# S4 tables and a sliding-window attention on one core: factors on GpSimd, absolute values by a mask, exponentials and sines in a fixed order, projections dealt over all table steps

## The chip, the cores and the metric

The kernel runs on one core of one Trainium2 chip. The core has five engines with queues of their own: PE (TensorE, matrix products into PSUM), DVE (VectorE), ACT (ScalarE, functions by activation tables), POOL (GpSimd) and SP (SyncE, which issues transfers), and 16 DMA engines. The metric is the device time of one execution in microseconds (us), the median of several runs.

## The reference

Two independent parts are computed and laid side by side in the output (2048 x 1152).

Part A is attention over a window: `qkv = x @ wqkv` with 2048 rows, 576 columns and 32 heads of 18, then for each row a softmax over itself and the 255 rows before it, and `o @ wo`.

Part B is a convolution by a state-space model, 576 channels with 128 states each:

```
dt = exp(log_dt);  logdA = dt * (A_re + i A_im);  dB = dt * (B_re + i B_im)
P[d, n, l] = exp(logdA[d, n] * l)                    l = 0 .. 2047
K[d, l]    = real( sum over n of C[d, n] * P[d, n, l] * dB[d, n] )
y          = causal convolution of u with K, per channel (by FFT), + u * Dskip
```

The exponent is complex, so each element of P needs an exponential (real part) and a sine and a cosine (imaginary part).

## The kernel before, in words

**Two stages.** The first stage computes, at the same time, the projections q, k, v (`proj`), the kernel K of the convolution (`tables`) and the first step of the transform of u (`s1_u`). When K is complete, `s1_k` transforms it and writes it to HBM (`gk`). The second stage runs attention and the rest of the convolution, in an order written out by hand.

**Tables.** The time index is split as l = 64 a + m, so that P is a product of two small tables. The 576 channels are worked in 18 groups of 32, here called pairs, each of two chunks of 16 channels (36 chunks, numbered c). For a pair there are factors A and tr (12 values of a per channel, with the weights C dB multiplied in); for a chunk there is Q (64 values of m, real and imaginary). The steps of one chunk:

- `outer` (L314): PE multiplies log-rates by index values and gives the exponents in PSUM, in one of two buffers (x).
- `exps_ab` (L334) and `exps_q` (L344): ACT takes exponentials of the real parts, for two pairs and four chunks at a time, into mab (3 buffers) and mg (4).
- `fraction` (L324 to L326): ACT rounds the phase to an integer k, DVE subtracts it (f), and ACT takes the absolute value ab with Abs. The sine of f and the cosine, as sine of pi/2 - |2 pi f|, follow on ACT (L356 and L357 for a pair, L395 and L396 for a chunk).
- `factors` (L358 to L369): six DVE operations make tr (768 elements per partition), t1 and t2 (256 each) and the three parts of A (128 each).
- `products` (L380): POOL multiplies A by tr into two tiles m of 1024 elements (pool P, two buffers of each).
- `qtable` (L400 to L403): DVE multiplies sines and cosines, which lie in PSUM, by mg into Q (two buffers).
- `taps` (L418): PE sums over the 128 states, 128 small matmuls a chunk as the trace counts them, into kp, one PSUM buffer for both chunks of a pair; ACT then copies kp into K (L424).

**Projections.** x comes in four column blocks. For each block ACT and DVE make a scaled half-precision pair xh and xl (L226 to L229); the scale needs the largest value of all of x, which goes over the partitions with an all-reduce on POOL (L144). Then there are nine steps for q and k (14 matmuls of width 512 each, L172, evicted by ACT at L236 and DVE at L237, six stores of about 0.6 us of issue on SP) and four for v (28 matmuls of width 288, evicted by ACT at L248, one store). They share three PSUM buffers (pps) with `s1_u` (L461). With the block's loading that makes 14 steps a block, 56 in all.

**What sets the order.** Every function is a Python generator that yields after a step, and `merge` picks the next step from the generator that has gone through the smallest share of the steps named for it:

```
merge((part(proj, 16), 16), (part(tables, 20), 20), (part(s1u, 4), 4))
merge((proj, 56), (tables, 400), (s1u, 12))
```

This gives a program order. A scheduler, which runs when the kernel is built, then fixes each engine's own queue from it: an instruction goes in as its inputs and its buffer become free by the scheduler's clock, earlier ones in the program first. On the chip every engine runs its queue strictly in that order. An activation table is loaded (ACT_TABLE_LOAD, 1.283 us) where an exponential follows a sine in ACT's queue, or a sine an exponential.

The number 400 in the second merge is the steps that `tables` is taken to have; it has 304 after the first 20.

Of the kernel before, what the change touches and what calls it, by code (L numbers as in the profile page):

```python
# [13 lines left out]
I32 = mybir.dt.int32  # L14
AF = mybir.ActivationFunctionType
OP = mybir.AluOpType
# [14 lines left out]
TWO_PI = 6.283185  # L31
# [71 lines left out]
class Kernel:  # L103
# [214 lines left out]
    def fraction(self, x, pool, n, w):  # L318

        nc = self.nc  # L320
        k = pool.tile([128, n * w], I32, name="k")
        f = k.bitcast(F32)
        ab = pool.tile([128, n * w], F32, name="ab")
        nc.scalar.activation(k, x, AF.Copy)  # L324
        nc.vector.tensor_tensor(f, x, k, op=OP.subtract)  # L325
        nc.scalar.activation(ab, f, AF.Abs)  # L326
        return f, ab

    def exps_ab(self, s):

        for q in (2 * s, 2 * s + 1):
            x = self.outer(self.al, q, [self.mul["c_ca"]], 0, GC)
            m = self.p["mab"].tile([128, GC, 12], F32, name="mab")
            self.nc.scalar.activation(m, x.rearrange("p (c m) -> p c m", m=12), AF.Exp)  # L334
            self.mab[q] = m
            yield

    def exps_q(self, s):

        for c in range(4 * s, 4 * s + 4):  # L340
            mg = self.p["mg"].tile([128, HC, 64], F32, name="mg")
            for e in range(2):
                x = self.outer(self.al, c // 2, [self.mul["c_cm"]], c % 2 * HC + e * 8, 8)
                self.nc.scalar.activation(mg[:, e * 8:e * 8 + 8], x.rearrange("p (c m) -> p c m", m=64), AF.Exp)  # L344
                yield
            self.mg[c] = mg

    def factors(self, q):

        nc, tt, pool = self.nc, self.nc.vector.tensor_tensor, self.p["ab"]  # L350
        x = self.outer(self.ps, q, [self.mul["c_ca"], self.mul["c_cp"]], 0, GC)
        f, ab = self.fraction(x, self.p["abt"], GC, 12)
        yield
        tr = pool.tile([128, GC, 2, 12], F32, name="tr")
        v = lambda z: z.rearrange("p (c m) -> p c m", m=12)
        nc.scalar.activation(tr[:, :, 1, :], v(f), AF.Sin, scale=TWO_PI)  # L356
        nc.scalar.activation(tr[:, :, 0, :], v(ab), AF.Sin, scale=-TWO_PI, bias=self.halfpi)  # L357
        tt(tr, tr, self.mab.pop(q).unsqueeze(2).to_broadcast([128, GC, 2, 12]), op=OP.mult)  # L358
        yield
        t1 = self.p["abt"].tile([128, GC, 2, 4], F32, name="t1")  # L360
        t2 = self.p["abt"].tile([128, GC, 2, 4], F32, name="t2")
        sh = [128, GC, 2, 4]
        w = lambda z: z[:, q * GC:q * GC + GC].unsqueeze(2).unsqueeze(3).to_broadcast(sh)
        tt(t1, tr[:, :, :, 8:12], w(self.wr), op=OP.mult)
        tt(t2, tr[:, :, :, 8:12], w(self.wi), op=OP.mult)
        A = pool.tile([128, GC, 12], F32, name="A")
        tt(A[:, :, 4:8], t1[:, :, 0], t2[:, :, 1], op=OP.subtract)
        tt(A[:, :, 8:12], t2[:, :, 0], t1[:, :, 1], op=OP.add)
        nc.vector.scalar_tensor_tensor(A[:, :, 0:4], t2[:, :, 0], -1.0, t1[:, :, 1], op0=OP.mult, op1=OP.subtract)  # L369
        self.AB[q] = A, tr  # L370
        yield

# [16 lines left out]
    def qtable(self, c):  # L389
        nc, tt = self.nc, self.nc.vector.tensor_tensor  # L390
        f, ab = self.fr.pop(c)
        sn = self.p["trig"].tile([128, HC, 32], F32, name="sn")
        cs = self.p["trig"].tile([128, HC, 32], F32, name="cs")
        v = lambda z: z.rearrange("p (c m) -> p c m", m=32)
        nc.scalar.activation(sn, v(f), AF.Sin, scale=-TWO_PI)  # L395
        nc.scalar.activation(cs, v(ab), AF.Sin, scale=-TWO_PI, bias=self.halfpi)  # L396
        yield
        m = self.mg.pop(c)
        Q = self.p["Q"].tile([128, HC, 2, 64], F32, name="Q")
        tt(Q[:, :, 0, 32:64], cs, m[:, :, 32:64], op=OP.mult)  # L400
        tt(Q[:, :, 0, 0:32], cs[:, :, ::-1], m[:, :, 0:32], op=OP.mult)  # L401
        tt(Q[:, :, 1, 32:64], sn, m[:, :, 32:64], op=OP.mult)
        nc.vector.scalar_tensor_tensor(Q[:, :, 1, 0:32], sn[:, :, ::-1], -1.0, m[:, :, 0:32],  # L403
                                       op0=OP.mult, op1=OP.mult)
        self.Q[c] = Q
# [20 lines left out]
    def tables(self):  # L426
        self.mab, self.mg, self.AB, self.P, self.fr, self.Q = {}, {}, {}, {}, {}, {}
        yield from self.exps_ab(0)
        yield from self.exps_ab(1)
        yield from self.exps_q(0)  # L430
        yield from self.factors(0)
        self.products(0)
        self.phases(0)
        yield
        n = 2 * NQ
        for c in range(n):
            if c % 2 == 0 and c // 2 + 1 < NQ:
                yield from self.factors(c // 2 + 1)
            if c + 1 < n:
                self.products(c + 1)  # L440
                self.phases(c + 1)
                yield
            yield from self.qtable(c)
            yield
            if c % 4 == 3 and c + 1 < n:
                if c + 5 < n:
                    yield from self.exps_ab(c // 4 + 2)
                yield from self.exps_q(c // 4 + 1)
            if c:
                yield from self.taps(c - 1)  # L450
        yield from self.taps(n - 1)


# [489 lines left out]
    def build(self):  # L943
        nc, a = self.nc, self.a
        with ExitStack() as es:
            self.pool(es, "const", 1)
            self.pool(es, "dram", 1, DRAM)
            self.pool(es, "dram2", 2, DRAM)
            cp, dp = self.p["const"], self.p["dram"]
            self.w1 = cp.tile([128, 2, 128], F32, name="w1")  # L950
            nc.gpsimd.dma_start(self.w1, a["c_w1"])
            self.gx = dp.tile([2, 64, 128, 144], F32, name="gx")
            self.gk = dp.tile([2, 64, 128, 144], F32, name="gk")
            self.h = dp.tile([2, 64, 32, D], F32, name="h")
            with ExitStack() as ek:
                self.pool(ek, "K", 1)
                with ExitStack() as e1:
                    for n, b, s in (("s4c", 1, None), ("pps", 3, PSUM), ("xps", 2, PSUM), ("trig", 1, PSUM),
                                    ("kps", 1, PSUM)):
                        self.pool(e1, n, b, s)  # L960
                    with ExitStack() as e2:
                        self.pool(e2, "prep", 1)
                        self.s4_prep()
                    for n, b in (("wq", 1), ("raw", 2), ("x", 1), ("pst", 2), ("s1u", 2), ("s1s", 2), ("ab", 2), ("abt", 1), ("mab", 3),
                                 ("mg", 4), ("fr", 2), ("Q", 2), ("P", 2)):
                        self.pool(e1, n, b)
                    proj, tables, s1u = self.proj(), self.tables(), self.s1_u()
                    merge((part(proj, 16), 16), (part(tables, 20), 20), (part(s1u, 4), 4))
                    merge((proj, 56), (tables, 400), (s1u, 12))
                with ExitStack() as e1:  # L970
                    self.pool(e1, "s1s", 2)
                    self.pool(e1, "s1p", 3, PSUM)
                    for _ in self.s1_k():
                        pass
            with ExitStack() as e1:
                self.pool(e1, "fc", 1)
                self.i2 = self.p["fc"].tile([128, 64], F32, name="i2")
                nc.sync.dma_start(self.i2, a["c_i2"])
                self.dsk = self.p["fc"].tile([128, D], F32, name="dsk")
                nc.sync.dma_start(self.dsk, a["dsk"].partition_broadcast(128))  # L980
                for n, b, s in (("fs", 2, None), ("fy", 2, None), ("att", 1, None), ("m", 2, None), ("P", 4, None),
                                ("v", 4, None), ("o", 3, None), ("n", 2, None), ("n1", 1, None), ("h7", 1, None), ("wo", 1, None), ("wo2", 2, None),
                                ("stp", 2, PSUM), ("ops", 1, PSUM), ("ring", 3, PSUM)):
                    self.pool(e1, n, b, s)
                self.att_setup()
                with self.tc.manual_schedule():
                    self.attention(self.conv())
# [35 lines left out]
```

## Time and profile before

| | |
|---|---|
| median of 3 runs | 1079.5 us (1076.2 to 1081.78) |
| the profiled execution | 1075.61 us, of which the span on the core is 1073.6 |
| PE busy | 857.8 us (80% of the span) |
| DVE busy | 736.2 us (69%) |
| ACT busy | 619.9 us (58%) |
| POOL busy | 511.1 us (48%) |
| mean granted clock of PE | 0.946 |
| ACT table loads from 30 to 475 us | 35, of 1.283 us each |

A busy share is an average over both stages and says little of either. PE's matmuls overlap in the pipeline and their ends are modelled, so a busy PE is not a PE at its peak; its real work is counted better from runs of back-to-back matmuls. The chain of waits follows the work that ended last backwards: at each step to what released it, or to the instruction before it on its engine. A row of one source line gives the shortest, median and longest duration in ns, the times of the first and last start, and the shape. A line of waits reads: who waited, for whom, us in total, how often, the longest.

### The profile page before, as it was taken

How to read it: one execution, taken by the hardware profiler on the slowest of the kernel's cores; microseconds unless marked ns; L12 is line 12 of the kernel's file. 1: busy time of each engine (PE TensorE's matmuls, PEld its weight loads, DVE VectorE, ACT ScalarE, POOL GpSimd, SP SyncE). 2: the span in 40 equal slices, each digit the busy share in tenths (PEclk: the TensorE clock that was granted, in tenths of full speed). 3: DMA queues.
4: the chain of work that ended last, by engine and by line, in shares of the span. 5: the costliest groups of instructions: out<-in, count | busy, mean ns of one | idle time of the engine just before them, and what ended most of it. 6: DMA issues, size and time to landing. Idle time of an engine off the chain costs nothing.

```text
span 1073.6 us, 26801 instructions
## 1 busy us (share of the span) xinstructions
PE 857.8 (80%) x10332; PEld 450.7 (42%) x10332; DVE 736.2 (69%) x1859; ACT 619.9 (58%) x955; POOL 511.1 (48%) x606
## 2 busy tenths in 40 slices
PE   1535879897988797987578888878888899988787
PEld 0313436554744464553234333333333344434345
DVE  2879685669576845226676788888878766767564
ACT  1776758776797784233146655566566656644471
POOL 0004344435452632010235677766876666666770
PEclk9966989998998998999889999999999999999999
DMA  9665423442344232588616456454645644579763
GB/s 271 168 184 160 105 53 88 109 94 59 85 111 96 55 74 64 130 217 239 188 49 180 138 147 175 147 148 127 176 113 177 185 118 142 146 185 256 204 190 121
DMA packets 155911, 152.27 MB, mean 142 GB/s; under 512 B 36856, under 2 KB 134392, under 8 KB 155592
## 3 DMA queue, kind: packets, MB, share of 16 engines
q1 hardware_dynamic: 148152, 131.98, 45.3%
q0 software_dynamic: 6128, 14.60, 5.4%
q10 hardware_dynamic: 1504, 3.99, 1.3%
q8 instruction: 81, 1.33, 0.6%
q14 instruction: 46, 0.38, 0.1%
HBM read 89.12 MB, written 61.01 MB: 140 GB/s over the span
## 4 chain that ended last, share of the span: by engine, by line
PE 37%; DVE 25%; ACT 10%; DMA 10%; issue 9%; POOL 5%; SPq 2%; DVEq 0%; ACTq 0%; POOLq 0%
PE pp L172 8%; PE r L636 4%; PE po L700 4%; PE r L903 4%; PE r L500 4%; PE kp L418 4%; PE pp L461 3%; DVE jk L643 3%; POOL P L688 2%; DMA gk<-g 2%; PE ST L677 2%; PE x L314 2%; PE r L508 2%; DVE tr L358 2%; ACT P L679 2%
## 5 line engine op out<-in xcount | busy, mean ns | idle before, releaser
L643 DVE CUSTOM_DVE_ANT_0 jk<-r,bias 128x288 f32<-128x288 f32 (+7 forms) x512 | 198.0, 433 | 88.7 <-PE r L636 88.0
L679 ACT ACTIVATE P<-ST,esc 128x1024 f32<-128x1024 f32 (+1 forms) x192 | 202.0, 1059 | 92.9 <-PE ST L677 92.1
L380 POOL TENSOR_TENSOR m<-A,tr 128x1024 f32<-128x1024 f32 x72 | 149.5, 2098 | 194.2 <-PE kp L418 139.1
L688 POOL TENSOR_SCALAR_AFFINE_SELECT P<-P 128x512 f32<-128x512 f32 x240 | 171.7, 745 | 103.2 <-ACT P L679 100.8
L636 PE MATMUL r<-K,qb 128*64 128x288 f16 (+7 forms) x1024 | 130.5, 297 | 36.7 <-DVE qb L627 10.7
L700 PE MATMUL po<-P,V 128*32 128x256 f32 (+2 forms) x1408 | 100.2, 395 | 17.5 <-POOL P L688 8.1
L418 PE MATMUL kp<-Q,m 128*32 128x64 f32 x4608 | 88.3, 230 | 27.6 <-DVE Q L401 10.0
L636 PEld LDWEIGHTS <-qb 128*64 128x64 f16 x1024 | 60.3, 109 | 119.3 <-issue 65.6
L536 POOL TENSOR_TENSOR Y<-t,t 64x288 f32<-64x288 f32 x64 | 53.5, 835 | 109.8 <-DVE t L531 107.8
L418 PEld LDWEIGHTS kp<-Q,m 128*32 128x32 f32 x4608 | 75.2, 116 | 56.3 <-issue 41.7
L461 PE MATMUL pp<-ut,w 128*128 128x288 f32 x128 | 52.8, 538 | 40.9 <-DMA ut<-in_u_dram 18.6
L677 PE MATMUL ST<-Q,K 64*128 64x384 f16 (+2 forms) x704 | 73.5, 280 | 3.0 <-DMA Q<-mt 2.9
L237 DVE SCALAR_TENSOR_TENSOR qst<-pp,qst 128x512 f16<-128x512 f32 x36 | 24.7, 685 | 64.7 <-ACT qst L236 61.8
L128 ACT ACTIVATE g<-pp 128x288 f32<-128x288 f32 (+1 forms) x84 | 34.5, 447 | 40.4 <-DMA gk<-g 22.0
L700 PEld LDWEIGHTS po<-P,V 128*32 128x32 f32 x1408 | 35.7, 110 | 52.5 <-issue 25.7
L537 POOL TENSOR_TENSOR Y<-t,t 64x288 f32<-64x288 f32 x64 | 54.5, 852 | 3.8
L461 PEld LDWEIGHTS pp<-ut,w 128*128 128x128 f32 x128 | 28.9, 245 | 61.1 <-issue 24.1
L326 ACT ACTIVATE ab<-k 128x512 f32<-128x512 f32 (+1 forms) x54 | 31.9, 590 | 37.0 <-DVE k L325 36.6
L172 PE MATMUL pp<-xh,wh 128*128 128x512 f16 x180 | 47.9, 388 | 1.2 <-DVE xh L229 1.2
L172 PEld LDWEIGHTS <-wh 128*128 128x128 f16 x324 | 32.0, 101 | 39.3 <-issue 6.6
L172 PE MATMUL pp<-xh,wl 128*128 128x512 f16 x180 | 48.3, 392 | 0.0
L500 PE MATMUL r<-tx,w 128*64 128x288 f32 x256 | 40.2, 430 | 9.9 <-DMA tx<-gx 8.7
(177 smaller groups left out, 1756.1 us busy)
## 6 DMA issues: line engine op xcount, KB each, us to landing
gx<-g SPq DMA_DIRECT2D x32, 288.0 KB
qd<-qst SPq DMA_DIRECT2D x72, 128.0 KB
gk<-g SPq DMA_DIRECT2D x16, 576.0 KB
tx<-gx SPq DMA_DIRECT2D x16, 576.0 KB
tk<-gk SPq DMA_DIRECT2D x16, 576.0 KB
h<-ho SPq DMA_DIRECT2D x16, 576.0 KB
raw<-in_xT_dram SPq DMA_DIRECT2D x16, 512.0 KB
Q<-qd SPq DMA_DIRECT2D x32, 216.0 KB
```

The lines of the kernel that those rows point to most:

```text
L172: self.nc.tensor.matmul(ps, u, v, start=(i == 0), stop=(i == len(ops) - 1))
L380: self.nc.gpsimd.tensor_tensor(m, A[:, ch, a0:a0 + 8].unsqueeze(3).to_broadcast(sh), tr[:, ch, part, 0:8].unsqueeze(2).to_broadcast(sh), o ...
L418: nc.tensor.matmul(kp[32 * st:32 * st + 32, c % 2 * JJ2 + j, :], m[:, ch, a0:a0 + 32], Q[:, ch, term % 2, :], start=(term == 0), stop=(ter ...
L461: nc.tensor.matmul(ps, self.w1[:, part, :], src[:, o:o + k], start=True, stop=True)
L500: nc.tensor.matmul(ps[64 * par:64 * par + 64], w2[:, par, 64 * part:64 * part + 64], t[:, 2 * hs:2 * hs + 2, par, :], start=True, stop=True)
L537: nc.gpsimd.tensor_tensor(Y[par][64:128], t1[sl, 1], t2[sl, 1], op=OP.add)
L636: nc.tensor.matmul(ps[64 * b:64 * b + 64, :n], self.qb[:, b, t, :], d["K"][:, b, k0:k0 + n], start=True, stop=True, skip_group_check=True)
L643: nc.vector.tensor_tensor_reduce(out=jk[:, :n], in0=ps[:, :n], in1=self.bias[:, 288 - n:], scale=1.0, scalar=-3e38, op0=OP.add, op1=OP.max ...
L677: nc.tensor.matmul(ps[:, u, o:o + n], d["K"][h, jp, k0:k0 + 128], d["Q"][h, jp, q0:q0 + n], start=True, stop=True, skip_group_check=True)
L679: nc.scalar.activation(pt[:, 2 * jp:2 * jp + 2, lo:hi], ps[:, :, lo:hi], AF.Exp, scale=self.esc)
L688: nc.gpsimd.affine_select(v, v, pattern=[[0, 4], [sg, 128]], compare_op=OP.is_ge, fill=0.0, base=-1 if far else 0, channel_multiplier=-sg)
L700: nc.tensor.matmul(self.po[32 * j:32 * j + 32, t0 * 128:t1 * 128], V[:, kb * 76 + 19 * j:kb * 76 + 19 * j + 32], pt[:, j, o:o + (t1 - t0) ...
```

## The change

It has five parts. In `fraction` the absolute value is no longer taken by ACT (Abs) but by DVE, as a bitwise mask that clears the sign. All exponentials and sines of the tables go through a helper `act`, which gives them a token that keeps them in program order on ACT. In `factors` the five two-input operations run on POOL in place of DVE, and the sixth, a scaled subtraction of two tiles, becomes the negative of the part just made (one input). `products(c + 1)` stands behind `taps(c - 1)` in the program, no longer ahead of `phases(c + 1)`. The pool mab has four buffers, and the merge is told 304 steps of tables instead of 400.

```diff
 def fraction(self, x, pool, n, w):
...
-        nc.scalar.activation(ab, f, AF.Abs)
+        nc.vector.tensor_scalar(ab.bitcast(I32), k, 0x7FFFFFFF, None, op0=OP.bitwise_and)
...
+    def act(self, *args, **kw):
+
+        self.tc.stamp_issue_order_token(self.nc.scalar.activation(*args, **kw).ins, "transcendentals")
...
 def exps_ab(self, s):
-            self.nc.scalar.activation(m, x.rearrange("p (c m) -> p c m", m=12), AF.Exp)
+            self.act(m, x.rearrange("p (c m) -> p c m", m=12), AF.Exp)
...
 def factors(self, q):
-        nc, tt, pool = self.nc, self.nc.vector.tensor_tensor, self.p["ab"]
+        nc, tt, pool = self.nc, self.nc.gpsimd.tensor_tensor, self.p["ab"]
...
-        nc.scalar.activation(tr[:, :, 1, :], v(f), AF.Sin, scale=TWO_PI)
-        nc.scalar.activation(tr[:, :, 0, :], v(ab), AF.Sin, scale=-TWO_PI, bias=self.halfpi)
+        self.act(tr[:, :, 1, :], v(f), AF.Sin, scale=TWO_PI)
+        self.act(tr[:, :, 0, :], v(ab), AF.Sin, scale=-TWO_PI, bias=self.halfpi)
...
-        nc.vector.scalar_tensor_tensor(A[:, :, 0:4], t2[:, :, 0], -1.0, t1[:, :, 1], op0=OP.mult, op1=OP.subtract)
+        nc.gpsimd.tensor_scalar(A[:, :, 0:4], A[:, :, 8:12], -1.0, None, op0=OP.mult)
...
 def tables(self):
             if c + 1 < n:
-                self.products(c + 1)
                 self.phases(c + 1)
...
             if c:
                 yield from self.taps(c - 1)
+            if c + 1 < n:
+                self.products(c + 1)
...
-                    for n, b in (("wq", 1), ("raw", 2), ("x", 1), ("pst", 2), ("s1u", 2), ("s1s", 2), ("ab", 2), ("abt", 1), ("mab", 3),
+                    for n, b in (("wq", 1), ("raw", 2), ("x", 1), ("pst", 2), ("s1u", 2), ("s1s", 2), ("ab", 2), ("abt", 1), ("mab", 4),
...
-                    merge((proj, 56), (tables, 400), (s1u, 12))
+                    merge((proj, 56), (tables, 304), (s1u, 12))
```

The other exponentials and sines (`exps_q`, `qtable`) go through `act` in the same way.

## The prediction

> **What bounds the kernel now.** I read the page first, for the engines' shares. None is full over the span (PE 80%, DVE 69%, ACT 58%), so the time has to be read by stage. The chain of waits around the end of the table stage comes next:
>
> ```profile
> 415.13 3.03 PE kp L418 x174
> 418.17 1.54 issue
> 419.71 0.52 PE kp L418 x18
> 420.23 12.19 PE pp L172 x56
> ...
> 434.65 15.11 PE pp L172 x70
> ...
> 452.00 7.03 PE pp L172 x56
> ...
> 459.49 7.33 DMA vd<-vst
> ...
> 467.66 5.38 DMA vd<-vst
> ...
> 473.58 3.50 DMA gk<-g
> ```
>
> Columns: start, length, what. The last taps (L418) end at 420.2. From there to 466 PE does nothing but projections (L172) and eight input transforms. Only then can the kernel's own transform (L461 on K, first matmul at 467.7) start. The engines by stretch:
>
> ```profile
> 102.90:420.30 317.40, 267.75 (x5273) 164.63 (x5272) 220.68 (x327) 235.52 (x403) 140.75 (x68) 0.93 0.36 85
> 420.30:467.70 47.40, 45.70 (x255) 25.88 (x253) 7.12 (x11) 11.69 (x24) 1.45 (x4) 1.00 0.60 131
> 467.70:521.50 53.80, 35.61 (x98) 17.67 (x98) 30.85 (x30) 16.36 (x36) 3.51 (x1) 0.91 0.85 241
> ```
>
> Columns: window, length, busy of PE, weight loads, DVE, ACT, POOL, then granted clock, DMA share, GB/s. The first row, from the first eviction of K to the last, holds 34 of the 36 chunks (17 pairs, 18.7 us each). The second is the tail: ACT and DVE are idle there, PE full. The third is bound by DMA (85% busy) and stays as it is, as does all behind 521.5. So the question is how long the first row gets when the second is folded into it.
>
> What is on the chain inside the first row? I summed its pieces by engine: PE 120 us, DVE 103, ACT 63. Of these, 47 us are DVE factor operations (L358 to L369), 7.6 the absolute values (L326) and 15 ACT table loads: 70 us on the chain are what this change removes or moves. Three rows say why the factors are so slow, and two what DVE holds up:
>
> ```profile
> L364 DVE TENSOR_TENSOR t<-tr,wr x18: 407/996/2066, 78.4 to 397.8; 128x256 f32<-128x256 f32 x18
> ```
> ```profile
> L237 DVE SCALAR_TENSOR_TENSOR qst<-pp,qst x36: 671/690/693, 113.2 to 452.5; 128x512 f16<-128x512 f32 x36
> ```
> ```profile
> L380 POOL TENSOR_TENSOR m<-A,tr x72: 1947/1957/2939, 80.1 to 407.6; 128x1024 f32<-128x1024 f32 x72
> ```
> ```profile
> PE x L314 <- DVE k L325: 19.3, 5, 6.1
> ...
> PE pp L461 <- DVE qst L237: 9.1, 2, 4.9
> ```
>
> The first three give min/median/max ns. L364 reads two SBUF tiles; alone it takes 0.41 us, but up to 2.07 when a POOL product (1.96) runs, and it ends when that does. L237 reads PSUM and never stretches. So DVE's SBUF work queues behind POOL, and the evictions that PE waits for queue behind DVE.
>
> **The change part by part.**
>
> *Projections over all table steps.* In the instruction list of the changed kernel all 952 projection matmuls (L172) stand ahead of the last taps; before, 238 stood behind them. Those are 126 at 0.2177 us (12.19/56) and 112 at 0.1255 (7.03/56): 41.5 us leave the tail. PE's work between the first projection and the last taps becomes: 504 x 0.2177 + 448 x 0.1255 = 166; 34 chunks of taps at 1.99 (one undisturbed run of 128) = 67.7; some 138 outer products (L314) at 0.21 (estimate from L172's width) = 29; some 80 input transforms at 2.39 per eight = 24. Sum 287 us at full clock, against 242 for the same stretch before. At the 0.93 granted there, 242 is 260, so PE stood still for 57 of 317 us. The moved steps also issue stores: 54 of queries and keys (issued 424.0 to 457.5, so 0.62 each on SP) and 8 of values (2.4 each). That is 53 us of SP's queue spread over some 320 us, and 6 MB on top of 27, or about 102 GB/s where the tail carried 131. I cost both at nothing; the cover is gone if the raw loads of the next columns, in the same queue, come late.
>
> *Factors to POOL.* DVE loses 4.65 us a pair (sum of the means of L358 to L369; 83.7 in all). POOL gains six operations: a line through L380 (1024 elements, 1.957) and the 64-partition L536 (288, 0.79) gives 1.55 for 768, 0.74 for 256, 0.54 for 128, so 1.55 + 1.48 + 1.08 + 0.5 = 4.6 us; from half that (DVE's undisturbed 2.6) to 6.9 (each stretched by L380's max over median). POOL then has 8.3 + 4.6 = 12.9 us a pair. It was idle half the time, mostly waiting for taps, so this hides.
>
> *Absolute values by a mask on DVE.* ACT loses 2 x 0.62 + 0.53 = 1.8 us a pair. No row shows a large one-input DVE operation in SBUF in this stage. From below 0.15 (L152, one element), from above 0.68 (L325, same width) plus a whole product of waiting, 2.07. I take 0.68 (0.55 for the narrow one) and 0.7 of waiting, as POOL is busy two thirds of the time and half a product is left on average: 4.0 us a pair. The copy L627 bears the waiting out: 643 ns at best, 1192 at worst, beside POOL's masks. What queues behind a mask on DVE are Q products and qst evictions, so PE is who would feel it.
>
> The Trainium skill (SBUF — State Buffer, Who interferes with whom) says why: DVE and GpSimd share one port pair under an exclusive lock, which a DVE operation with two SBUF inputs, or a tensor_scalar in a two-port mode, holds or waits for whole. It speaks against this change, since both new kinds of work meet in that lock. L364 and L237 agree with it. By the rule's worst, one product per mask, DVE would need 16.7 us a pair, still under PE's.
>
> *Fixed order of exponentials and sines.* The lists hold 37 table loads before and 19 after: 18 x 1.283 = 23 us off ACT. ACT is not the bound after it; the 15 us that were on the chain go. What may be late instead: sines behind a block of ten exponentials (about 8.5 us every second pair, as 10 x 0.58 + 2 loads); PE has 28 to 56 projections (6 to 12 us) to run meanwhile.
>
> *Products behind the taps, one more mab buffer.* P has two buffers, so products waited for the taps anyway: nothing. But POOL's all-reduce of the x scale (L144), which all projections wait for, now stands behind 17 POOL operations instead of four, and the scale behind two more chunks' Q products on DVE. First projection before: 101.6. I take 105, from 101.6 to 112 (a pair more at the low clock there).
>
> **Sum.** Clock midway between 0.93 and the 1.00 of the tail: 287/0.965 = 297 us. Standing still: of the 57, the 19.3 and 9.1 above are DVE's, which is freed of 84 us and given some 70, none of it as long; they go, leaving 28. Last taps: 105 + 297 + 28 = 430; K's eviction (1.03) and start-up: 431.3 instead of 467.7. Gain 36.4. Check of the others over these 325 us: DVE 221 - 79 + 68 + 6 = 216, ACT 236 - 30 - 23 + 12 = 195, POOL 141 + 78 = 219. None binds. The profiled execution took 1075.6, so 1039; the median shown is 1079.5, 3.9 above it, so **1043** on that scale, which I use from here.
>
> **Rivals.**
> - *PE runs free*: clock 1.00, 10 us of standing still: 105 + 287 + 10 = 402, gain 64, 1015. For: PE's list mixes 14 to 28 projections between any two taps. Against: the clock rows at 0.86 even in busy stretches.
> - *The tail is folded in and given back*: all 57 us remain at 0.93: 105 + 309 + 57 = 471, no gain, 1084. For: in-order queues; masks hold Q and qst as the factors did. Against: 70 us of the chain are gone.
> - *Slower: masks locked out by POOL*. If a mask waits for both products of a chunk (4.2 us), DVE needs 8.7 + 3 x 4.2 + 1.9 = 23.2 us a pair, last taps at 499, 1112. It decides from 21.3 us a pair ((467.7 - 1.3 - 105)/17), so from 3.5 us of waiting a mask. Against: no stretched row above exceeds one product, 2.07. For: POOL's queue is now much denser, and chained operations wait for one another in both directions.
> - *It does not do what it says*: excluded by the lists.
>
> **Chances.** Forecast (standing still 12 to 45 us, 1027 to 1060) 0.58; PE free 0.12; given back, wholly or mostly (1060 to 1085) 0.18; slower 0.12. A measurement tells 0.5% (5.4 us) from no change. Faster: 0.58 + 0.12 + half of 0.18 = 0.79; same 0.09; slower 0.12. The range 1016 to 1080 leaves out some 0.05 below and 0.15 above.
>
> **What the changed profile would show.** Right: last taps near 430 with no L172 behind them, first L461 on K just after, PE over 90% busy between at 0.95 or more, POOL near 65%, mask means 0.7 to 1.4 us, 19 table loads. Wrong: PE waiting for Q or k with DVE in L326 beside POOL; or projections starting after 112; or the stretch from the first L461 on K to the attention growing beyond 54 us, because stores pile up there.

## The result, and the profile after

The changed kernel took 1049.3 us (median of 4 runs, 1041.8 to 1052.7) against 1080.6 for the kernel before: a ratio of 0.9715, 95% interval 0.9686 to 0.9744. A second set of runs of the same kernel (further down) gave 0.9656 (0.9598 to 0.9713). The forecast was 1043 us, with a range of 1016 to 1080. The profiled execution took 1041.77 us; the forecast on the scale of the profile was 1039. It was the fastest of its four, 7.5 us below their median.

The end of the table stage in the chain of waits, in the same columns as before (start, length, what; the taps are L422 now, the transforms L466):

```profile
415.41 1.92 PE kp L422 x128
417.34 3.54 PE pp L172 x28
420.88 3.09 PE kp L422 x201
...
427.51 0.88 PE kp L422 x20
428.41 1.04 ACT K L428
429.50 4.22 PE pp L466 x6
```

No projection stands behind the last taps, and the first transform of K starts at 429.5 instead of 467.7. The engines by stretch (window, length, busy PE, weight loads, DVE, ACT, POOL, clock, DMA share, GB/s):

```profile
97.30:428.40 331.10, 300.09 (x5530) 185.07 (x5530) 199.03 (x301) 205.41 (x364) 211.50 (x169) 0.97 0.43 102
...
429.50:483.30 53.80, 36.37 (x96) 17.89 (x96) 28.74 (x28) 16.13 (x36) 0.90 (x1) 0.91 0.78 231
483.30:1040.10 556.80, 471.08 (x4386) 221.41 (x4386) 407.67 (x1412) 297.71 (x421) 352.88 (x520) 0.97 0.55 154
```

The first row, from the first eviction of K to the last, is 331 us now with all projections in it; before, it was 317 with 47 of tail behind. ACT and DVE each lost work, POOL went from 44% to 64%. The stretch behind, bound by DMA, is 53.8 us as before. The mask and two of the moved operations, by source line (min/median/max ns):

```profile
L326 DVE TENSOR_SCALAR ab<-k x54: 342/467/2150, 68.4 to 416.2; 128x512 int32<-128x512 int32 x36, 128x384 int32<-128x384 int32 x18
```
```profile
L362 POOL TENSOR_TENSOR tr<-tr,mab x18: 1797/1832/3642, 69.5 to 404.1; 128x768 f32<-128x768 f32 x18
```
```profile
L368 POOL TENSOR_TENSOR t<-tr,wr x18: 622/632/897, 73.2 to 406.0; 128x256 f32<-128x256 f32 x18
```

A mask takes 0.34 us at best and 0.47 by the median, but up to 2.15 beside a POOL instruction: it waits like the factors did. All 21 masks longer than 0.6 us end 0.2 to 0.3 us behind the end of a POOL instruction, as the nine long ones of L364 did in the kernel before (0.28 us). All 54 take 42 us.

To compare kernels I use one measure from here on: the stretch from the first projection to the first transform of K, the clock granted in it, and the time in which PE stands still, which is the stretch less 287 us (PE's work, from the prediction) over the clock. It is good to a few us: the clock's second digit is worth 3 us, and some kernels do a chunk of taps (2 us of PE) more or less ahead of the stretch. For the kernel before and the changed one:

```profile
101.60:467.70 366.10, 314.75 (x5532) 191.05 (x5530) 229.07 (x339) 248.51 (x428) 142.54 (x72) 0.94 0.39 91
```
```profile
105.80:429.50 323.70, 298.26 (x5513) 184.37 (x5512) 192.91 (x285) 199.35 (x356) 212.23 (x168) 0.98 0.44 104
```

366.1 - 287/0.94 = 61 us of standing still before; 323.7 - 287/0.98 = 31 after. So of the 42 us, 30 are standing still and 12 the higher clock.

### The profile page after: what moved, and what is told of

Same layout as the page of the kernel before. It is cut to its first block, busy times and chain, and to the rows that moved or that the text cites. A ratio compares the mean times of both kernels' runs of the same rounds, so it can differ in the third digit from the quotient of the medians.

```text
span 1040.1 us, 26776 instructions
## 1 busy us (share of the span) xinstructions
PE 842.3 (81%) x10332; PEld 443.0 (43%) x10332; DVE 703.1 (68%) x1805; ACT 569.9 (55%) x883; POOL 593.5 (57%) x714
## 4 chain that ended last, share of the span: by engine, by line
PE 40%; DVE 21%; DMA 12%; issue 10%; ACT 7%; POOL 7%; SPq 2%; DVEq 0%; ACTq 0%; POOLq 0%
PE pp L172 11%; PE r L641 4%; PE kp L422 4%; PE r L505 4%; PE po L705 4%; PE r L908 4%; DVE jk L648 3%; PE pp L466 3%; POOL P L693 3%; PE x L314 2%; DMA gk<-g 2%; PE ST L682 2%; DVE qb L632 2%; ACT P L684 2%; PE r L513 2%
## 5 line engine op out<-in xcount | busy, mean ns | idle before, releaser
L384 POOL TENSOR_TENSOR m<-A,tr 128x1024 f32<-128x1024 f32 x72 | 145.6, 2045 | 86.8 <-PE kp L422 79.6
L422 PE MATMUL kp<-Q,m 128*32 128x64 f32 x4608 | 80.6, 224 | 16.5 <-issue 6.1
L422 PEld LDWEIGHTS kp<-Q,m 128*32 128x32 f32 x4608 | 70.4, 112 | 38.8 <-issue 26.6
L466 PE MATMUL pp<-ut,w 128*128 128x288 f32 x128 | 47.8, 506 | 42.6 <-DMA ut<-in_u_dram 25.4
L325 DVE TENSOR_TENSOR k<-x,k 128x512 f32<-128x512 f32 (+1 forms) x54 | 33.9, 638 | 39.1 <-ACT k L324 39.0
L362 POOL TENSOR_TENSOR tr<-tr,mab 128x768 f32<-128x768 f32 x18 | 34.7, 1929 | 31.1 <-ACT tr L331 31.1
L466 PEld LDWEIGHTS pp<-ut,w 128*128 128x128 f32 x128 | 26.5, 227 | 58.2 <-ACT g L128 17.5
L172 PEld LDWEIGHTS <-wh 128*128 128x128 f16 x324 | 31.6, 99 | 45.7 <-issue 12.4
```

Source lines behind the costliest of these rows:

```text
L172: self.nc.tensor.matmul(ps, u, v, start=(i == 0), stop=(i == len(ops) - 1))
L384: self.nc.gpsimd.tensor_tensor(m, A[:, ch, a0:a0 + 8].unsqueeze(3).to_broadcast(sh), tr[:, ch, part, 0:8].unsqueeze(2).to_broadcast(sh), o ...
L422: nc.tensor.matmul(kp[32 * st:32 * st + 32, c % 2 * JJ2 + j, :], m[:, ch, a0:a0 + 32], Q[:, ch, term % 2, :], start=(term == 0), stop=(ter ...
L466: nc.tensor.matmul(ps, self.w1[:, part, :], src[:, o:o + k], start=True, stop=True)
```

## Experiments: which part of the change does it

The theory on record (A) was that PE's work is the same and relief of DVE and ACT lets PE stand still less; its rival (B), that the gain is the folding of the tail. The first four kernels set them against each other: one does one part alone, three undo one part each.

**Dealing alone.**

```diff
 (before)
-                    merge((proj, 56), (tables, 400), (s1u, 12))
+                    merge((proj, 56), (tables, 304), (s1u, 12))
```

> The kernel before with one number changed: the merge is told 304 table steps instead of 400, so that all projections stand ahead of the last taps. Theory A (relief): PE's work of 287 us is the same in both kernels; what fell is the time in which PE stands still between the first projection and the first transform of K (58 us before, 27 after), and that falls because DVE and ACT are relieved. Dealing alone leaves the standing still at some 55 us: first transform of K at 458 to 466, 1068 to 1078 us. Theory B (dealing): the gain is the folding of the tail in which only PE worked; dealing alone gives nearly all of it: first transform of K near 432, 1045 to 1055 us.

Measured: 1070.2 us, ratio 0.9902 (0.9872 to 0.9931).

```profile
102.60:454.70 352.10, 307.16 (x5531) 186.87 (x5529) 230.43 (x342) 260.78 (x438) 141.42 (x73) 0.97 0.41 96
```

The tail is gone, yet PE stands still 56 us of 352, against 61. In this profile the gain is mostly the clock, 0.97 against 0.94, and the first transform of K, at 454.7, is sooner than the 458 expected; but it is the fastest of ten executions, 7 us below their median. The time, 10.5 us below that of the kernel before, is what theory A expected.

**Everything but dealing.**

```diff
 (after)
-                    merge((proj, 56), (tables, 304), (s1u, 12))
+                    merge((proj, 56), (tables, 400), (s1u, 12))
```

> The changed kernel with the merge told 400 steps again: 238 projection matmuls stand behind the last taps, all other parts of the change stay. Theory A (relief): the tables end near 385 to 395, the tail of 46 us follows at full clock, first transform of K at 431 to 441: 1047 to 1062 us. Theory B (dealing): the tail stands on top of a table stage that is hardly shorter than before, first transform of K at 460 or later: 1070 to 1080 us.

Measured: 1055.7 us, ratio 0.9784 (0.9720 to 0.9848). K's last eviction is at 393.5 and the tail of projections follows, up to the first transform of K at 441.3. The tail is still there and most of the gain too: theory A again. PE stands still 41 us of 333.7 (clock 0.98), 10 more than in the changed kernel, so dealing is not without use there: by the medians it is worth 6 us against the first set of the changed kernel, where the intervals overlap, and 13 against the second (0.9656), where they just do not.

**Absolute values back on ACT.**

```diff
 (after, in fraction)
-        nc.vector.tensor_scalar(ab.bitcast(I32), k, 0x7FFFFFFF, None, op0=OP.bitwise_and)
+        nc.scalar.activation(ab, f, AF.Abs)
```

> The changed kernel with the absolute values back on ACT. ACT gets 32 us of work back (205 of 331 us in the stage becomes 237), DVE loses 42. Theory A: ACT has room, the masks were no part of the gain: 1044 to 1054 us. Rival C (the mask relieved ACT where it counted): 1060 us or more. Rival D (the masks meet POOL in the lock and cost): DVE rid of waits of up to 2.1 us, 1036 to 1043 us.

Measured: 1037.8 us, ratio 0.9625 (0.9589 to 0.9662): rival D. ACT takes the absolute values back without harm, and PE stands still 24 us:

```profile
109.20:425.90 316.70, 296.82 (x5400) 182.87 (x5399) 158.60 (x240) 221.58 (x402) 205.78 (x167) 0.98 0.45 107
```

The masks were no gain but a cost (how large, further down).

**Factors back on DVE.**

```diff
 (after, in factors)
-        nc, tt, pool = self.nc, self.nc.gpsimd.tensor_tensor, self.p["ab"]
+        nc, tt, pool = self.nc, self.nc.vector.tensor_tensor, self.p["ab"]
...
-        nc.gpsimd.tensor_scalar(A[:, :, 0:4], A[:, :, 8:12], -1.0, None, op0=OP.mult)
+        nc.vector.scalar_tensor_tensor(A[:, :, 0:4], t2[:, :, 0], -1.0, t1[:, :, 1], op0=OP.mult, op1=OP.subtract)
```

> The changed kernel with the six factor operations back on DVE. Theory A: DVE's load in the stage grows from 199 to some 278 of 331 us, with waits of up to 2 us behind POOL's products ahead of the evictions that PE needs; PE stands still 15 to 25 us more: 1062 to 1075 us. Theory B: dealing and order are in place, so 1045 to 1054 us.

Measured: 1083.1 us, ratio 1.0033 (1.0012 to 1.0053). Beyond what theory A expected: without this part the change is a small loss.

```profile
105.90:474.80 368.90, 317.16 (x5660) 193.34 (x5658) 254.39 (x396) 206.85 (x366) 142.46 (x73) 0.93 0.39 92
```

Still 60 us, at a clock of 0.93, although DVE is busy only 254 of 369 us. Busy shares do not show this bound. Waits do: PE waits for DVE's results here as it did in the kernel before (a line reads: who waited, for whom, us in total, how often, the longest).

```profile
PE x L314 <- DVE k L325: 17.0, 6, 4.6
...
PE kp L422 <- DVE Q L405: 14.3, 6, 3.7
```

**The order of exponentials and sines.** Two kernels leave the token out, one with the masks, one with the absolute values on ACT:

```diff
-        self.tc.stamp_issue_order_token(self.nc.scalar.activation(*args, **kw).ins, "transcendentals")
+        self.nc.scalar.activation(*args, **kw)
```

> The changed kernel without the token that keeps exponentials and sines in program order: its list holds 45 table loads instead of 19, 33 us more on ACT. Theory A (only what frees DVE counts, ACT has room: 199 of 324 us): PE stands still at most 10 us longer, 1047 to 1060 us. Rival E (the order is a part of the gain): 15 us or more longer, 1063 us and up.

> The changed kernel with the absolute values on ACT and without the token (43 table loads): of the change, the factors on POOL, the dealing, the place of the products and the fourth mab buffer are left. ACT then has some 222 + 31 of 317 us. Theory A: 1037 to 1050 us. Rival E (the order counts once ACT carries the absolute values): 1053 us and up.

Measured: 1051.5 us, 0.9730 (0.9704 to 0.9757), and 1038.1 us, 0.9597 (0.9570 to 0.9624). Each agrees with its partner that has the order (0.9715 and 0.9625). 24 to 26 table loads more, 31 to 33 us of ACT at 1.283 us each, cost nothing that can be told: theory A. With the masks a few us are not excluded: the second set of the changed kernel lies 9 us lower, its interval only just overlaps, and PE stands still 38 us here against 31. The fourth mab buffer belongs to this part: in program order the four first exponentials all stand ahead of the first sine, whose factors free a buffer.

**Factors alone.** The edit of e4 the other way round, on the kernel before, and nothing else:

> The kernel before with the six factor operations on POOL and nothing else. Theory A, sharpened by the first four runs (the factors' waits on DVE behind POOL's products are the cause): PE's standing still falls from 61 to some 40 us and the clock rises to 0.97, first transform of K at 443 to 450: 1056 to 1064 us. Rival F (the parts help only together: freed of the factors alone, DVE and ACT are still held up): 1068 to 1080 us.

Measured: 1041.9 us, ratio 0.9621 (0.9583 to 0.9660), well below what I expected.

```profile
107.20:431.60 324.40, 301.79 (x5400) 183.25 (x5399) 157.07 (x236) 238.59 (x415) 202.34 (x166) 0.98 0.44 103
```
```profile
L364 POOL TENSOR_TENSOR t<-tr,wr x18: 627/632/640, 76.6 to 361.0; 128x256 f32<-128x256 f32 x18
```

One part gives as much as the whole change. The last taps start at 381.9 (420 before), the full tail follows, and the first transform of K starts at 431.6. PE stands still 31.5 us, as in the changed kernel. The same operation that took DVE 0.41 to 2.07 us takes POOL 0.63 to 0.64. PE's waits for DVE are nearly gone: the 19.3 us for k of the kernel before are 0.6, and the largest that is left is one of 2.7 us for Q. All waits of PE's matmuls for DVE in the stretch sum to 35 us before, 41 with the factors back on DVE (e4), 13 in the changed kernel and 6 here. That is the path by which the rows show the factors to hold up PE. In the kernel before, the 108 factor operations take 83.7 us of DVE; at the shortest time of each line they would take 46, so 37 are waiting beside POOL. On POOL (e8) they take 82.8 us, and only 2.0 of them are above the shortest times. How much of the gain comes from the 37 us of waiting and how much from the 46 of plain work that DVE loses, no run separates.

No other part adds a gain on top that can be told: with dealing, moved products, the fourth mab buffer and the absolute values on ACT it is 1038.1 (e7), whose interval overlaps this one. The masks are a loss.

**The first projection.** On e3_abs_act, POOL's all-reduce is replaced:

```diff
 def pow2_max(self, parts, nm):
-        nc.gpsimd.partition_all_reduce(g, m, 128, bass.bass_isa.ReduceOp.max)
+        nc.vector.tensor_copy(mb, m.to_broadcast([128, 128]))
+        ps = self.p["xps"].tile([128, 512], F32, name="x")
+        nc.tensor.matmul(ps[:, :128], mb, self.ident1, start=True, stop=True)
+        nc.vector.tensor_reduce(g, ps[:, :128], axis=AX.X, op=OP.max)
```

> The kernel with the absolute values on ACT (e3_abs_act), and the largest values of x and w taken over the partitions by a matmul with the identity and a DVE maximum in place of POOL's all-reduce. It tests the term of the first projection: in the changed kernel POOL stood idle 6.0 us before the all-reduce of x and 7.2 after it, with nothing in the profile that it waited for. Theory A with that term: the first projection starts at 96 to 101 instead of 109, PE's stretch after it stays: 1026 to 1033 us. Rival G (the start is hidden: the tables, not the projections, set the pace after it): 1035 to 1039 us.

Measured: 1039.6 us, 0.9619 (0.9589 to 0.9650): rival G by the time, a little above its range. The first projection starts at 102.2 instead of 109.2, but the stretch behind it is 325.6 instead of 316.7 us: the first three chunks' taps, which PE did before the projections in e3, now lie within it (some 6 us). The seven us were moved, not won.

**What a mask costs: lock or load?** On e3_abs_act, 54 spare operations on DVE that nothing reads, one kind with the lock, one without:

```diff
 (in fraction, behind the Abs on ACT)
+        sp = self.p["abt"].tile([128, 512], I32, name="spare")[:, :n * w]
+        nc.vector.tensor_scalar(sp, k, 0x7FFFFFFF, None, op0=OP.bitwise_and)
```
```diff
+        sp = pool.tile([128, 1], F32, name="spare")
+        nc.vector.tensor_reduce(sp, f, axis=AX.X, op=OP.max)
```

> The kernel with the absolute values on ACT (e3_abs_act) plus 54 spare masks on DVE, from k into a scratch tile that nothing reads. The masks of the changed kernel cost 11 us (1049 against 1038). Theory L (the lock: a mask on DVE waits for POOL's instruction and holds up the Q products and evictions behind it, and POOL's waits for the mask): the spare masks cost the same without any sine waiting for them, 1045 to 1053 us, with a longest mask near 2.1 us. Rival C (the chain: ACT's cosine waits for the mask): nothing waits here, 1036 to 1042 us.

> The kernel with the absolute values on ACT plus 54 spare reductions on DVE (maximum along the row of f, 0.68 us for 512 elements, into one column that nothing reads). The reductions of x (1471 to 1489 ns) never stretched beside POOL, so this is DVE load of some 34 us without the lock. Theory L: 1036 to 1042 us. Rival M (plain DVE load and queueing, not the lock, is what the masks cost): 1046 us or more.

> The changed kernel once more, beside the two above on the same chip: 1044 to 1054 us, 8 us or more above e3_abs_act, so that the cost of the masks does not rest on runs of different calls.

> The kernel with the absolute values on ACT once more (the same as e3_abs_act), with more rounds, as the changed kernel gave ratios of 0.9715 and 0.9656 to the kernel before in two sets of runs. If the masks cost something (theory L), its ratio is 0.958 to 0.965 again. If it comes out at 0.967 or more, the cost of the masks inside the whole change isn't established by these two kernels, and rests on the pairs with and without masks elsewhere.

Measured: spare masks 1046.1 us, 0.9696 (0.9661 to 0.9731); spare reductions 1042.9, 0.9664 (0.9627 to 0.9702); the changed kernel 1042.8, 0.9656 (0.9598 to 0.9713); absolute values on ACT 1036.8, 0.9604 (0.9577 to 0.9631).

```profile
L328 DVE TENSOR_SCALAR spare<-k x54: 345/544/2157, 69.6 to 423.1; 128x512 int32<-128x512 int32 x36, 128x384 int32<-128x384 int32 x18
```
```profile
L328 DVE TENSOR_REDUCE spare<-k x54: 535/676/686, 70.0 to 415.6; 128x1 f32<-128x512 f32 x36, 128x1 f32<-128x384 f32 x18
```

The rows show the lock plainly: the mask reaches 2157 ns, the reduction never more than 686. In time, masks that nobody waits for cost as much as real ones (rival C falls: 0.9696 against 0.9604, intervals apart; the first set of the kernel without them, 0.9625, touches it at 0.9662). But the reduction, without the lock, lies between, above the 1042 us of theory L and below the 1046 of rival M, and its interval overlaps both. In the profiles PE stands still 34 us with the spare masks, 26 with the spare reductions and 26 without either (e3, with one chunk of taps less in PE's work). That speaks for the lock, but it is one profile of each. How much of the masks' cost is waiting and how much is plain queueing on DVE stays open. The changed kernel's second set, expected at 1044 us or more, came out at 1042.8, and its interval overlaps with that of ACT too, so inside the whole change the cost of the masks is 6 to 12 us by the medians. It is clear in the first set, and clear in two other pairs, though these carry the order token and the place of the products along: with the projections not dealt (e2 against e8, 0.9784 and 0.9621) and with the factors on DVE (e4 against e1, 1.0033 and 0.9902).

**The better version.** The change with the absolute values left on ACT has the lowest times: 1037.8 us (0.9625) and 1036.8 us (0.9604, interval 0.9577 to 0.9631) in two sets of runs. Both intervals are clear of the first set of the changed kernel and overlap with the second. The simplest one, factors on POOL alone, reaches 1041.9, and the two cannot be told apart by their intervals.

## Why the prediction was right

- *First projection*, forecast 105: measured 105.8, and 107.6 in the second profile of the same kernel (e12). The delay came as argued: POOL is done with what stands ahead of the all-reduce at 94.7 instead of 88.5. The gap of 6 to 7 us that follows in both kernels (last section) had not been seen, and does not explain the difference.
- *PE's work, 287 us, and the clock*, forecast 0.965: 0.98 over the stretch, some 5 us better than taken. The work was 2.4 us more, as the trace has 88 matmuls of input transforms in the stretch and the sum took some 80. Midway was a choice, and that it came near is partly luck: the clock was 0.93 and 0.94 in the two stretches with some 60 us of standing still and 0.97 to 0.99 in all others, but one of these others (e1) has 56 us of it at 0.97. What sets it is open.
- *Standing still falls from 57 to 28*: 61 to 31 by the measure above, so neither rival on it (10 us left, or all 57) came true. This was the term that decided. Its reason was that PE's waits on evictions and outer products come from DVE being held by factors that queue behind POOL's products. e4 and e8 bear it out: the factors' engine alone switches between 60 and 31 us, and the waits for DVE come and go with it. Of the 19.3 and 9.1 us that were to go, 6.9 are left in the changed kernel:

```profile
PE x L314 <- DVE k L325: 3.6, 5, 1.5
...
PE pp L466 <- DVE qst L237: 3.3, 2, 3.0
```

- *First transform of K*, forecast 431.3: 429.5.
- *Nothing changes behind it*: the profiled gain is 33.8 us where the first transform came 38.2 sooner. The 4.7 us (556.8 instead of 552.1) are scatter of the second stage: over the profiles taken here, first transform to end lies between 606 and 613 us for every kernel, with no relation to the change.
- *The factors on POOL*, forecast 4.6 us a pair: 34.7 + 14.7 + 11.8 + 10.6 + 9.3 + 8.6 = 90 us over 18 pairs, 5.0. Hidden, as POOL still waited 80 us for taps.

The signs that the prediction named were there too: PE is busy 300 of 331 us, POOL 64%, the mean mask takes 0.78 us, and the list has 19 table loads.

Three steps were off, and the sum came out near because they are small or cancel:

- "So the question is how long the first row gets when the second is folded into it" framed the gain as dealing. Dealing alone is worth 1.0% (e1). With the moved products and the fourth buffer it adds nothing that can be told to the factors (e7 against e8), and in the whole change it is worth 6 to 13 us by the medians (e2). The tail was hardly lost time: PE was busy 45.7 of its 47.4 us, and PE has the same work either way.
- "None binds" for the masks, with 4.0 us of DVE a pair at no cost. They took 2.3 (42.1 us over 18 pairs), less than forecast, and yet cost time. The rival "masks locked out by POOL" had the right place, but its price was far too high: the longest mask waited for one POOL instruction (2.15 us), never two. The sentence that both new kinds of work meet in the lock holds where both are there: beside the masks, 9.5 of the factors' 89.7 us on POOL are above the shortest times. Without the masks the factors on POOL hardly stretch (2.0 of 82.8 us in e8), so for them the lock speaks for the move, not against it.
- "The 15 us that were on the chain go", for the fixed order. The loads went from 35 to 17 in the stage and no gain can be told (e5, e7); what lies on the chain of waits is not yet what its removal saves.

The Trainium skill has a rule against the part that made the gain: GPSIMD Engine Reference, Engine selection, puts elementwise work of two inputs on VectorE, as GpSimd is about twice as slow. The rows agree on the bare operation, at 1.5 times for 256 elements (0.63 us against 0.41) and twice for 768 (1.83 against 0.94, the shortest of L358). The measurement decides otherwise for the kernel: e8 is 3.8% faster with it.

## What to carry to other kernels

In this kernel an operation of DVE that reads two SBUF tiles, or a mask that reads one, took as long as the POOL instruction beside it let it (0.41 to 2.07 us, and 0.34 to 2.15), and the evictions queued behind it waited too; look at min and max of its row, not at busy shares. If the POOL queue has room, putting such operations into it, in line with the very products they used to wait for, can be worth more than the slower engine costs, as it was here. And before work is dealt from a stretch with one full engine into another, count that engine's work over both: where it is the same, only its standing still can be won.

## What the runs showed of the hardware

POOL's all-reduce of x came with two gaps that its inputs do not explain: in the changed kernel 6.0 us before it (the scale's maximum was ready at 91.9, POOL free at 94.7, the all-reduce started at 100.7) and 7.2 us from its end to the next product; with the factors alone (e8) they were 6.4 and 7.0. A POOL configuration instruction (MODIFY_POOL_CONFIG) stands in each gap. In the kernel before they were 6.9 and 6.8 us, but there the maximum was ready only at 93.3, 2.1 us ahead of the all-reduce, so that part of the first may be waiting for it. So the scale came later than its place in the queue alone would make it, and in e9, without the all-reduce, the projections start 7 us sooner than in e3. The Trainium skill (GPSIMD Engine Reference, Instruction dispatch) tells of some 6 us for loading the code of a kernel that was not resident, with no instruction to see. The first gap agrees with that. The second suggests that the way back costs as much; no run here tests it by itself.

On POOL the time of a product with a broadcast operand was not a matter of elements alone: 768 elements took 1.83 us (L362) and 1024 took 1.95 (L384), while 256 took 0.63 (L368). And the negative of 128 elements with one input (0.53, L373) was slower than a difference of two tiles of that width (0.46, L371).
